# A spectral-mixing FFN kernel: bank rotation in the first FFT, a new order of loads, z in two runs of partitions

## Chip, cores and metric

One Trainium2 chip, one core of it. The metric is the device time of one execution in microseconds (us). A kernel's time is the median of its runs. Times within a run are counted from the start of the profiled span. PE is TensorE, PEld its weight loads, DVE VectorE, ACT ScalarE, POOL GpSimd, SP the engine that issues most transfers. The granted clock is the share of full speed that PE is given; 0.50 is called half clock here. All the runs compared below were in the fast state.

## The reference

```python
X = np.fft.rfft(x, axis=1)                 # x: (8, 3008, 256) float32
Y = X * (filt_r + 1j * filt_i)[None]       # filters: (1505, 256)
y = np.fft.irfft(Y, n=3008, axis=1).astype(np.float32)
h = np.maximum(y.reshape(24064, 256) @ w_in, 0.0)    # w_in: (256, 2048)
out = (h * h @ w_out).astype(np.float32)             # w_out: (2048, 256)
```

## The kernel before

The FFT of length 3008 = 64 x 47 is a chain of matrix products in half precision. **A** makes u from x (47-point part), u goes out to HBM and comes back in another order, **B** does the 64-point part, VectorE multiplies by the filter ("product"), **P** is the inverse 64-point part, z goes out and comes back, **Y** is the inverse 47-point part. **F** brings the filter into the order of B's output by products with permutations. The FFN then runs over 47 groups of 512 tokens, each in 8 slots: a slot does one eighth of the first layer of one group (psH), squares it on VectorE, and one eighth of the second layer of the group before (psO). The FFTs of the seven other batches are laid into these slots by a plan. Only the first batch's FFT stands alone, ahead of the slots; that is the prologue.

The parts that matter (cuts marked `# ...`). Pools first. A pool has slots too, its buffers, which tiles take in turn; these are meant where the text speaks of a slot of a pool, or of a tile's slot. `p_h2` has two of them and many guests, one after the other:

```python
p_h2 = ctx.enter_context(tc.tile_pool(name="p_h2", bufs=2))
# guests of p_h2, in order of their first use: third piece of x(0); u0 (all of u of
# batch 0); f16 (filter in half precision); win32 (first FFN weight, float32);
# wout32 (second FFN weight, float32); from then on the hidden tiles h2

def place_f(im, k, eng):                    # F, one sixth of one filter half
    ps = psH(f"psf_{im}_{k}")               # one of two double banks
    # ... 8 or more permutation products into ps, then one eviction by eng
```

The prologue:

```python
load_f(0)                                   # filt_r, right behind x
# ... constants, chunk_a: A over the same two double banks
chunk_a(0, 0); chunk_a(0, 2); write_u(0, 0); write_u(0, 2)
load_f(1)                                   # filt_i
chunk_a(0, 1); chunk_a(0, 3); write_u(0, 1); write_u(0, 3)
# load sSB; read_u(0); load sSP
f16s.append(p_h2.tile([128, 2, QF + D], F16, tag="h2", name="f16"))
# ... two small casts of the Nyquist row into it, on GpSimd
for im, eng in enumerate((nc.gpsimd, nc.vector)):
    # ... cast filter half im into f16 on eng
    for k in range(6):
        place_f(im, k, nc.vector if k % 2 else nc.scalar)
    keep_warm(12)
# load x(1,0), x(1,1); four half-width swapped copies of sSP on GpSimd; cast x on GpSimd
for r in range(14):
    if r < 12: unit_b(0, r)                 # B and the product
    if r >= 2: unit_p(0, r - 2)             # P; every third one writes a piece of z
    if r == 7: load_win(); cast_win()
for c in range(4): read_z(0, c)             # 96 partitions each
load_wout(); load_x(1, 2); load_x(1, 3)
cast_wout()                                 # four casts on GpSimd
# ... A of x(1,0), x(1,1); casts of x(1,2), x(1,3) on GpSimd
keep_warm(14)
for n in range(16): unit_y(0, n)
```

In the plan for batch b + 1, the casts of its four x pieces are put on VectorE; for batch 2 at slots 31, 33, 35 and 37 of batch 1's plan, each of the first two followed by the request for the next piece but one.

Of the kernel before, what the change touches and what calls it, by code (L numbers as in the profile page):

```python
# [19 lines left out]
QF = 3008  # L20
# [3 lines left out]
def _build_consts():  # L24
# [57 lines left out]

    SY = np.zeros((NC, 2, 2, N2, 2))
    for c in range(NC):
        th = 2 * np.pi * c * n2 / N2
        for i in range(2):
            SY[c, i, 0, :, i] = np.cos(th)
            SY[c, i, 1, :, i] = -np.sin(th)

# [9 lines left out]
    C0[0:94, 576:672] = SA.reshape(94, 96)  # L99
    C0[0:96, 672:766] = SY.reshape(96, 94)  # L100
    return f16(C0, 128), f16(PF, 128), f16(SB, 128), f16(SP, 128)
# [3 lines left out]
def kernel(  # L105
# [34 lines left out]
    p_ze = ctx.enter_context(tc.tile_pool(name="p_ze", bufs=3))  # L140
    p_zt = ctx.enter_context(tc.tile_pool(name="p_zt", bufs=4))
    p_y = ctx.enter_context(tc.tile_pool(name="p_y", bufs=2))
# [17 lines left out]

    prologue = [True]


# [20 lines left out]
    sSA = sC0[0:94, 576:672]  # L184
    sSY = sC0[0:96, 672:766]
    sPF = p_zt.tile([128, 6, 128], F16, tag="zt", name="sPF")
    nc.scalar.dma_start(out=sPF, in_=dPF.ap().rearrange("p (w q) -> p w q", q=128))
# [13 lines left out]
    def load_f(im):  # L201
        filt = filt_i if im else filt_r
        t = p_y.tile([128, QF], F32, tag="yt", name=f"f32_{im}")
        nc.sync.dma_start(out=t, in_=filt[0:1504, :].rearrange("a d -> (a d)").rearrange("(p e) -> p e", e=QF))
        f32s.append(t)

    load_f(0)
    nyq = p_out.tile([128, 2, D], F32, tag="ost", name="nyq")
    nc.gpsimd.memset(nyq, 0.0)
# [23 lines left out]

    def place_f(im, k, eng):

        ps = psH(f"psf_{im}_{k}")
        for i in range(4):
            c = 4 * k + i
            e0, e1 = D * c, D * (47 - c)
            cuts = [0] + [d for d in range(1, D) if (e0 + d) % QF == 0 or (c and (e1 + d) % QF == 0)] + [D]  # L240
            for d0, d1 in zip(cuts, cuts[1:]):
                o = ps[:, i // 2, (i % 2) * D + d0:(i % 2) * D + d1]
                q, a = divmod(e0 + d0, QF)
                nc.tensor.matmul(o, sPF[:, PQ.index((0, q)), :], f16s[0][:, im, a:a + d1 - d0],  # L244
                                 start=True, stop=False)
                q, a = divmod(e1 + d0, QF) if c else (0, QF + d0)
                nc.tensor.matmul(o, sPF[:, PQ.index((1, q)), :], f16s[0][:, im, a:a + d1 - d0],
                                 start=False, stop=True)
        dst = sF[:, im, 4 * k:4 * k + 4, :]
        src = ps.rearrange("p t (a d) -> p (t a) d", d=D)  # L250
        if eng is nc.scalar:
            eng.activation(out=dst, in_=src, func=AF.Copy, scale=sign[:, 0:1] if im else 1.0)
        elif im:
            eng.tensor_scalar_mul(out=dst, in0=src, scalar1=sign[:, 0:1])
        else:
            eng.tensor_copy(out=dst, in_=src)

# [16 lines left out]

    def cast_wout():
        for k in range(4):
            nc.gpsimd.tensor_copy(out=sWout[:, 4 * k:4 * k + 4, :],
                                  in_=w32s[1][:, 4 * k:4 * k + 4, :])

# [30 lines left out]
    def chunk_a(b, c):  # L310
# [6 lines left out]
        for k in range(2):  # L317
            ps = psH(f"psA_{b}_{c}_{k}")
            for i in range(2):
                m = slice(4 * k + 2 * i, 4 * k + 2 * i + 2)  # L320
                o = ps[0:96, i, :]
                if b == 0:
                    nc.tensor.matmul(o, s0[:, c // 2, :], x016[2 * (c % 2)][:, m, :],  # L323
                                     start=True, stop=False)
                    nc.tensor.matmul(o, s0[0:120, 2 + c, :], x016[1][0:120, m, :],  # L325
                                     start=False, stop=True)
                else:
                    nc.tensor.matmul(o, sSA, x16s[(b, c)][:, m, :], start=True, stop=True)
            o = u[:, 4 * k:4 * k + 4, :]
            pv = ps[0:96].rearrange("p t (a d) -> p (t a) d", d=D)  # L330
            if k == 0:
                nc.scalar.copy(out=o, in_=pv)
            else:
                nc.vector.tensor_copy(out=o, in_=pv)

# [33 lines left out]
    def unit_p(b, p):  # L369
# [16 lines left out]
        if i6 == 2:  # L386
            nc.sync.dma_start(
                out=dZ[b].rearrange("(s p) d -> p s d", p=128)[:, 6 * c:6 * c + 6, :],
                in_=zes.pop((b, c)))

    def read_z(b, c):
        zt = p_zt.tile([96, 8, D], F16, tag="zt", name=f"zt_{b}_{c}")
        nc.sync.dma_start(
            out=zt, in_=dZ[b].rearrange("(q j) d -> q j d", j=NM)[:, 8 * c:8 * c + 8, :])
        zts[(b, c)] = zt
# [3 lines left out]
    def unit_y(b, n):  # L399
# [9 lines left out]
        else:  # L409
            if dt == 0:  # L410
                yps[0] = psH(f"psY_{b}_{n}")
            ps = yps[0][:, dt, :]
        for jj in range(4):
            nc.tensor.matmul(ps[:, 94 * jj:94 * jj + 94],  # L414
# [56 lines left out]
    def fft_plan(b):  # L471
# [5 lines left out]

        for a in range(16):
            if b == 1 and a < 8:
                continue  # L480
            r = 2 + a // 2 if b == 1 else a // 2
            put(r, a % 2, unit_a, b, a)
        put(10 if b == 1 else 8, 1, read_u, b)
        for p in range(12):
            r = 14 + p if b == 1 else 13 + 19 * p // 11
            put(r, 0, unit_b, b, p)
            put(r + (b == 1), b == 1, unit_s, b, p)
            put(r + 2 + (b == 1), 1, unit_p, b, p)
        for c in range(4):
# [24 lines left out]
    for k, eng in enumerate((nc.vector, nc.vector, nc.gpsimd)):  # L514
        for i in range(2):
            m = slice(4 * i, 4 * i + 4)
            eng.tensor_copy(out=x016[k][:, m, :], in_=x0[k][:, m, :])
    chunk_a(0, 0)
    chunk_a(0, 2)
    write_u(0, 0)  # L520
    write_u(0, 2)
    load_f(1)
    chunk_a(0, 1)
    chunk_a(0, 3)
    write_u(0, 1)
    write_u(0, 3)
    nc.sync.dma_start(out=sSB, in_=dSB.ap().rearrange("p (a b) -> p a b", b=128))
    read_u(0)
    nc.sync.dma_start(out=sSP, in_=dSP.ap().rearrange("p (a b) -> p a b", b=128))

# [3 lines left out]
    for im, eng in enumerate((nc.gpsimd, nc.vector)):  # L534
        for e in (slice(0, 1504), slice(1504, QF)):
            eng.tensor_copy(out=f16s[0][:, im, e], in_=f32s[im][:, e])
        for k in range(6):
            place_f(im, k, nc.vector if k % 2 else nc.scalar)
        keep_warm(12)
    for c in range(2):  # L540
        load_x(1, c)

    for k in range(2):
        t = p_u.tile([128, 12, 128], F16, tag="u", name=f"sSPx_{k}")
        c = slice(12 * k, 12 * k + 12)
        nc.gpsimd.tensor_copy(out=t[0:64], in_=sSP[64:128, c, :])
        nc.gpsimd.tensor_copy(out=t[64:128], in_=sSP[0:64, c, :])
        sSPx.append(t)
    for c in range(2):
        cast_x(1, c, nc.gpsimd)  # L550
    for r in range(14):
        if r < 12:
            unit_b(0, r)
        if r >= 2:
            unit_p(0, r - 2)
        if r == 7:
            load_win()
            cast_win()
    for c in range(4):
        read_z(0, c)  # L560
    load_wout()
    for c in range(2):
        load_x(1, c + 2)
    cast_wout()
    for c in range(2):
        chunk_a(1, c)
        write_u(1, c)
        cast_x(1, c + 2, nc.gpsimd)
    keep_warm(14)
    for n in range(16):  # L570
# [51 lines left out]
```

## Time and profile before

| | before |
|---|---|
| time, median of 3 runs | 826.12 us (825.33 to 826.16) |
| PE busy in the profiled span of 825.9 us | 793.3 us (96%) |
| first matmul of F | 22.35 us |
| first product of B | 41.74 us |
| last write of z landed | 62.49 us |
| first matmul of Y that uses z | 66.73 us |
| second-layer product of slot 9 | 94.06 us |

The prediction shows the page and the order of instructions of this kernel. Two more pieces are needed later. In a table of busy time by stretch (stretch, length, busy time of PE, PEld, DVE, ACT, POOL with the number of instructions, granted clock, DMA share, GB/s), the 43 us in which F, B and P run:

```profile
19.00:39.00 20.00, 17.78 (x135) 12.37 (x135) 10.52 (x10) 8.43 (x8) 0.00 (x0) 1.00 0.93 314
39.00:62.00 23.00, 17.30 (x106) 9.93 (x103) 17.26 (x15) 8.95 (x14) 11.29 (x8) 1.00 0.71 211
```

And in the order of instructions (start, length, engine, line, operation, tiles, and in brackets the idle time before with what ended it), the casts on GpSimd and the wait of VectorE for x(2,2):

```profile
77.46 4.91 POOL L277 CAST sWout<-wout 128x1024 f16<-128x1024 f32 x4 [13.19 <-DMA wout<-in_moe_w_out_dram]
...
152.03 1.22 DVE L285 CAST x<-x 94x2048 f16<-94x2048 f32 x1 [2.15 <-DMA x<-in_x_dram]
```

PE is busy and at full clock in the first table. The weight's cast waits 13.19 us for a transfer. The last line is VectorE standing 2.15 us at a cast in the middle of the slots.

### The profile page before, as it was taken

Reading aid. Unit: us, or ns where it says so; the run is one execution under the profiler, and the core shown is the slowest. Engines: PE = TensorE matmul, PEld = TensorE weight load, DVE = VectorE, ACT = ScalarE, POOL = GpSimd, SP = SyncE. Lnnn points to the kernel's source line nnn. Section 1 sums busy time; section 2 is a strip of 40 time slices with the busy share of each in tenths; the row PEclk is TensorE's granted clock in tenths of the full one; section 3 lists DMA queues with packets and bytes.
Section 4 is the critical chain, followed back from the end, with each engine's and each line's share of the span. In section 5 each row is a group of like instructions: output and inputs, shape, how many; then the busy total and the mean of one; then the engine's idle time right before and its main releaser. Section 6 shows DMA issues by size and latency. Waiting matters only on the chain.

```text
span 825.9 us, 14241 instructions
## 1 busy us (share of the span) xinstructions
PE 793.3 (96%) x5960; PEld 551.4 (67%) x5960; DVE 551.5 (67%) x861; ACT 548.0 (66%) x695; POOL 50.3 (6%) x53
## 2 busy tenths in 40 slices
PE   6876899999999999999999999999999999999998
PEld 2643466667777676676767776776767767676666
DVE  2573697659965699557975599557985599544432
ACT  2343667677777677676777677776777777666664
POOL 3143263000000000000000000000000000000000
PEclk8996999999999999999999999999999999999999
DMA  7969427544562455334671545534572432411111
GB/s 274 325 205 259 114 92 200 152 130 147 143 169 73 145 154 144 112 99 138 156 208 46 172 122 147 141 84 134 139 185 83 118 120 70 128 40 39 39 39 52
DMA packets 88576, 110.23 MB, mean 133 GB/s; under 512 B 4040, under 2 KB 79560, under 8 KB 83912
## 3 DMA queue, kind: packets, MB, share of 16 engines
q1 hardware_dynamic: 88160, 108.94, 45.4%
q8 instruction: 46, 0.75, 0.4%
q10 hardware_dynamic: 288, 0.39, 0.2%
q14 instruction: 18, 0.15, 0.1%
q0 software_dynamic: 64, 0.00, 0.0%
HBM read 59.51 MB, written 49.81 MB: 132 GB/s over the span
## 4 chain that ended last, share of the span: by engine, by line
PE 85%; DMA 6%; DVE 5%; issue 2%; ACT 1%; SPq 0%; DVEq 0%; ACTq 0%
PE psO L459 37%; PE psH L444 36%; PE psY L414 3%; PE psA L299 3%; DMA x<-in_x_dram 2%; PE psB L346 2%; PE psP L382 2%; DMA zt<-dZ 2%; DVE prod L349 2%; DMA dZ<-ze 1%; DVE h L452 1%; PE psA L323 1%; PE psA L325 1%; DMA ut<-dU 0%; PE psf L244 0%
## 5 line engine op out<-in xcount | busy, mean ns | idle before, releaser
L448 ACT ACTIVATE h<-psH 128x1024 f16<-128x1024 f32 x376 | 385.2, 1025 | 197.9 <-PE psH L444 191.2
L444 PE MATMUL psH<-yt,sWin 128*128 128x512 f16 (+7 forms) x1728 | 389.6, 353 | 0.9 <-DVE yt L423 0.5
L459 PE MATMUL psO<-sWout,h 128*128 128x256 f16 x3008 | 389.5, 273 | 0.0
L459 PEld LDWEIGHTS <-h 128*128 128x128 f16 x3008 | 291.3, 98 | 76.9
L452 DVE TENSOR_TENSOR h<-h 128x1024 f16<-128x1024 f16 x376 | 263.4, 710 | 113.8 <-ACT h L448 113.5
L444 PEld LDWEIGHTS <-sWin 128*128 128x128 f16 x1728 | 160.5, 98 | 106.0 <-issue 8.6
L349 DVE TENSOR_TENSOR prod<-psB,sF 128x1024 f16<-128x1024 f32 x96 | 116.1, 1219 | 6.0 <-PE psB L346 5.2
L384 ACT CAST ze<-psP 128x512 f16<-128x512 f32 x96 | 56.3, 586 | 30.4 <-PE psP L382 17.7
L423 DVE CAST yt<-psY 128x376 f16<-128x376 f32 x64 | 35.2, 549 | 61.1 <-PE psY L414 61.0
L306 DVE CAST u<-psA 96x512 f16<-96x512 f32 x52 | 35.7, 686 | 49.5 <-PE psA L299 49.5
L466 ACT COPY ost<-psO 128x512 f32<-128x512 f32 x94 | 55.3, 589 | 6.8 <-PE psO L459 5.8
L414 PEld LDWEIGHTS <-zt 96*128 96x128 f16 x512 | 36.2, 104 | 25.3 <-DMA zt<-dZ 8.0
L414 PE MATMUL psY<-sC,zt 96*128 96x94 f16 x512 | 42.9, 215 | 9.0 <-DMA zt<-dZ 5.3
L299 PE MATMUL psA<-x,sC 94*96 94x512 f16 x104 | 39.9, 385 | 2.4 <-DVE u L306 2.3
L346 PE MATMUL psB<-ut,sSB 128*128 128x256 f16 x192 | 36.4, 272 | 5.9 <-DVE prod L349 5.2
L346 PEld LDWEIGHTS <-sSB 128*128 128x128 f16 x192 | 18.7, 98 | 29.3 <-issue 10.1
L421 ACT CAST yt<-psY 128x376 f16<-128x376 f32 x64 | 29.9, 467 | 11.7 <-PE psY L414 11.7
L364 DVE TENSOR_TENSOR yf<-prod,yf 128x512 f16<-128x512 f16 x84 | 35.5, 423 | 3.0 <-POOL yf L358 0.5
L382 PE MATMUL psP<-yf,sSP 128*128 128x256 f16 x168 | 32.1, 273 | 0.0
L285 DVE CAST x<-x 94x2048 f16<-94x2048 f32 x24 | 29.2, 1217 | 2.1 <-DMA x<-in_x_dram 2.1
L304 ACT CAST u<-psA 96x512 f16<-96x512 f32 x52 | 29.7, 572 | 0.0
L357 DVE COPY yf<-prod 64x512 f16<-64x512 f16 x72 | 20.8, 289 | 2.5
(48 smaller groups left out, 225.5 us busy)
## 6 DMA issues: line engine op xcount, KB each, us to landing
out_dram<-ost SPq DMA_DIRECT2D x94, 256.0 KB, 3.8
x<-in_x_dram SPq DMA_DIRECT2D x24, 768.0 KB, 6.2
dU<-u SPq DMA_DIRECT2D x32, 384.0 KB, 3.4
dZ<-ze SPq DMA_DIRECT2D x32, 384.0 KB, 2.9
zt<-dZ SPq DMA_DIRECT2D x32, 384.0 KB, 5.9
ut<-dU SPq DMA_DIRECT2D x8, 1024.0 KB, 6.2
ut<-dU SPq DMA_DIRECT2D x8, 512.0 KB, 3.7
x<-in_x_dram SPq DMA_DIRECT2D x3, 1024.0 KB, 7.4
```

Source lines behind the costliest of these rows:

```text
L299: nc.tensor.matmul(ps[0:96, :], sSA, x16s[(b, c)][:, 2 * i:2 * i + 2, :], start=True, stop=True)
L306: nc.vector.tensor_copy(out=o, in_=pv)
L346: nc.tensor.matmul(ps[:, i * D:(i + 1) * D], sSB[:, 2 * p + i, :], uts[b][:, 2 * p + i, :], start=True, stop=True)
L349: nc.vector.tensor_mul(out=prod, in0=ps.rearrange("p (a d) -> p a d", d=D).unsqueeze(1).to_broadcast([128, 2, 2, D]), in1=sF[:, :, 2 * p:2 ...
L382: nc.tensor.matmul(ps[:, i * D:(i + 1) * D], sSP[:, c2, :], prod[:, i, :], start=True, stop=True)
L384: nc.scalar.copy(out=zes[(b, c)][:, 2 * i6:2 * i6 + 2, :], in_=ps.rearrange("p (a d) -> p a d", d=D))
L414: nc.tensor.matmul(ps[:, 94 * jj:94 * jj + 94], zt[:, 4 * (g % 2) + jj, dt * 128:(dt + 1) * 128], sSY, start=True, stop=True)
L444: nc.tensor.matmul(ps[:, i, o:o + n], sWin[:, dt, jt * 128:(jt + 1) * 128], yts[b][:, dt, r:r + n], start=(dt == 0), stop=(dt == 1))
L448: nc.scalar.activation(out=h2[:, 2 * s:2 * s + 2, :], in_=ps, func=AF.Relu)
L452: nc.vector.tensor_mul(out=v, in0=v, in1=v)
L459: nc.tensor.matmul(pso[g][:, t % 2, :], h2s[g][:, jt, t * 128:(t + 1) * 128], sWout[:, jt, :], start=(jt == 0), stop=(jt == NJT - 1))
L466: nc.scalar.copy(out=ost, in_=pso[g])
```

## The change

The intent: keep PE from waiting for evictions in the prologue (four pairs of banks in rotation), have all of F's input ahead of u on the queue, spread the constants and weights so that what is needed first comes first, take the second weight's casts from GpSimd to VectorE slot by slot, read z onto partitions 0 to 47 and 64 to 111, and fill Y's waits with products by zeros. The diff, cut:

```diff
+    def bank_pair(name):          # double banks of psH twice, then psF pair, psO pair
+        k = npair[0] % 4
+        # ... A (chunk_a) and F (place_f) take their banks from here and evict
+        #     in turn by ScalarE and VectorE
     load_f(0)
+    load_f(1)
-    chunk_a(0, 0); chunk_a(0, 2); write_u(0, 0); write_u(0, 2); load_f(1); ...
+    for c in (0, 2, 1, 3):
+        chunk_a(0, c)
+        write_u(0, c)
+    # sSB and sSP loaded in halves: SB0, SP0, read_u(0), SB1, SP1
+    load_win()
+    for c in range(2):
+        load_x(1, c)
     f16s.append(p_h2.tile([128, 2, QF + D], F16, tag="h2", name="f16"))
     # ... filter casts and F, as before
-        keep_warm(12)
-    for k in range(2):                       # swapped copies of sSP
+    for k, eng in enumerate((nc.vector, nc.gpsimd)):
-        nc.gpsimd.tensor_copy(...)  # twice
+        eng.tensor_copy(...)        # twice
+    cast_win()
-        if r == 7: load_win(); cast_win()
-    cast_wout()                              # GpSimd
+    # plan of batch 1: cast_wout(k) on VectorE at slots 2 to 5, x(1,2), x(1,3) cast
+    # on VectorE at slots 6 and 7; A, read_u, B a slot later
-    keep_warm(14)
+    keep_warm(12)
     def read_z(b, c):
-        one transfer onto 96 partitions
+        for k in range(2):
+            nc.sync.dma_start(out=zt[64 * k:64 * k + 48],
+                              in_=v[48 * k:48 * k + 48, 8 * c:8 * c + 8, :])
     # Y contracts over 112 partitions (16 of them zeros); in unit_y:
+        if prologue[0]:
+            nc.tensor.matmul(ps[:, 0:D], zero[:, 0:128], zero[:, 0:D], start=True, stop=True)
```

## The prediction

> **What bounds the kernel now.** I read the page first, then the table of busy time by stretch, the order of instructions of the first 110 us, and the waits. The page's slices and the table say where time can be lost at all:
>
> ```profile
> PE   6876899999999999999999999999999999999998
> PEclk8996999999999999999999999999999999999999
> ```
>
> ```profile
> 62.00:67.00 5.00, 0.27 (x4) 0.27 (x5) 0.00 (x0) 0.00 (x0) 2.27 (x3) 0.94 0.68 169
> 67.00:75.00 8.00, 5.76 (x64) 4.97 (x63) 3.94 (x8) 3.78 (x8) 0.00 (x0) 0.50 1.07 296
> 81.00:90.00 9.00, 6.12 (x26) 2.36 (x25) 8.64 (x8) 6.17 (x8) 5.96 (x4) 1.00 0.42 119
> ...
> 150.00:300.00 150.00, 148.73 (x1161) 104.48 (x1159) 108.30 (x178) 107.03 (x139) 0.00 (x0) 1.00 0.46 131
> 300.00:500.00 200.00, 199.77 (x1543) 143.25 (x1542) 149.37 (x250) 144.31 (x185) 0.00 (x0) 1.00 0.49 136
> ```
>
> (Stretch, its length, busy time of PE, weight loads, VectorE, ScalarE, GpSimd, granted clock, DMA share, GB/s.) From 150 us on PE is busy 99 to 100% at full clock. The change adds no PE work there: the products with zeros are issued in the prologue alone, and contracting over 112 instead of 96 rows streams the same 94 columns. So all that can move lies in the first 100 us: the first batch's forward FFT (stages A, F and B), its inverse (P, the z read, Y), and the first eight half-filled FFN slots. The order of instructions there:
>
> ```profile
> 14.48 0.74 POOL L533 CAST f<-nyq 128x256 f16<-128x256 f32 x2
> ...
> 22.35 0.27 PE L244 MATMUL psf<-f,sPF 128*128 128x256 f16 x1
> ...
> 30.73 0.81 SPq L340 DMA_DIRECT2D ut<-dU  x2
> ...
> 41.74 13.67 DVE L349 TENSOR_TENSOR prod<-psB,sF 128x1024 f16<-128x1024 f32 x12 [1.59 <-PE psB L346]
> ...
> 62.63 1.73 SPq L393 DMA_DIRECT2D zt<-dZ  x4
> ...
> 66.73 1.12 PE L414 MATMUL psY<-sC,zt 96*128 96x94 f16 x12 [4.87 <-DMA zt<-dZ]
> ...
> 81.36 6.74 DVE L452 TENSOR_TENSOR h<-h 128x1024 f16<-128x1024 f16 x4 [0.88 <-ACT h L448]
> ...
> 94.06 1.04 PE L459 MATMUL psO<-sWout,h 128*128 128x256 f16 x8
> ```
>
> The reader should see four things. F (line 244) starts at 22.3, right behind A. The twelve products of B take 13.7 us on VectorE in one piece, so VectorE, not PE, paces B and P. PE then waits 4.87 us for z. And four squarings that cost 0.69 us each are spread over 6.74 us at 81 us, while GpSimd casts the second weight and x. The last line is the second-layer product of slot 9; from there slots follow at some 1.75 us, as in the steady state. I measure the prologue to this point.
>
> **What the Trainium skill says.** (1) "TensorE: Matmul & The Clock Gate", Part 1: the clock falls to half after about 3.4 us of idling and rises after about 3.4 us of sustained work. The trace agrees: the 128x512 matmuls of A follow each other at 0.22 us, then at 0.43 us, after the idling from 6.3 to 10.6 us; the clock of 67 to 75 us is 0.50 after the wait for z. (2) "SBUF — State Buffer", "Who interferes with whom": a VectorE instruction with two SBUF inputs blocks against a GpSimd instruction that reads SBUF. The stretched squarings beside GpSimd casts agree. (3) The same page, "Can I just issue two DMAs to hit both halves?", answers no (two transfers at partitions 0 and 64 gained 6%). The trace has only the single-piece form: 128-row reads ran at some 400 GB/s, the 96-row z read at some 255. Whether two runs of 48 help is not shown here.
>
> **The change, part by part.** All times are from the start of the span.
>
> *A over four bank pairs.* Before, PE waited for the eviction of the pair in use (1.31 us at 14.05), and that gap seems to have kept the clock at half until 18.6. With four pairs the gap goes. A's first product with both inputs stays at 10.6, since it waits for x. 32 matmuls: about 20 at 0.43 and the rest at 0.22 at worst, and at best half of them slow; PE ends A about 19 to 20 instead of 22.2, the last eviction about 20.5 instead of 23.6. The evictions of split pairs are 2 x 0.57 us (ScalarE) or 2 x 0.69 us (VectorE) for 1.01 and 1.22: no bound.
>
> *Filter loads ahead of u.* The first filter half landed at 15.9, and the second, 1.54 MB at the 400 GB/s that the queue showed, would be in at 19.5 instead of 28.4. The four u writes (0.39 MB, about 1.1 us each in line) follow it and have landed about 24.5. Before, the read of u waited for them until 30.7. So u is in SBUF 6 us earlier, at about 30.5. But that is not what sets B's start.
>
> *The weights' buffer.* This is the step that I rate highest. The first FFN weight is now requested before the half-precision filter copy, from the same two-slot pool. The slot that came free first, that of the third x piece, now goes to the weight; the filter copy gets the slot of u, free only once all u writes have landed. Before, the filter cast at 14.48 began as soon as the x cast had ended, which agrees with its having that slot. So F can start at 24.5 + 0.74 + 2.83 (two filter casts of GpSimd, from the groups) = 28.1, not 22.35: 5.8 us later. PE idles from 20 to 28 and comes back at half clock.
>
> *F itself.* 54 matmuls per filter half: 42 x 0.108 and 12 short ones make 5.2 us at full clock, and with four pairs the evictions (1.02 to 1.28 us, alternating between two engines) keep up. First half: 5.2 + 2.0 for the cold stretch, to 35.3. Then, as before, VectorE must evict its last block (1.3) and cast the second filter (2 x 0.93), to 38.5; the dummy matmuls that filled this gap are gone, so the second half may start cold: 5.2 + 1.5, to 45.2. Last eviction 1.4 and the two swapped weight copies now on VectorE, some 0.9: the first product is at 47.5 instead of 41.7. **Lost: 5.8 us.**
>
> *B, P, z.* Twelve products 13.7 us, to 61.2; 1.3 more to the last z write (as before, 55.4 to 56.7), at 62.5. That write took 5.76 us before because the weight load was ahead of it on the queue; this load now runs near 35 us, so I take the usual 2.9: 65.4. Reading z: 4.05 us to the first tile, as before (twice as many issues, half the bytes each). Y starts at 69.5 instead of 66.7. **Net loss to here 2.8 us.**
>
> *From Y to slot 9.* Before, 94.06 - 66.73 = 27.3 us. The fillers make Y longer while cold (16 x 0.088 + 4 x 0.216 + a wait of 0.56 = 2.8 us per four units, against 1.97) and shorter later; I take 8 us for 8.7. The casts that blocked VectorE leave GpSimd: 4 x 0.65 us for the second weight and 2 x 1.22 for x, in VectorE's own order. The new limit is VectorE after the second weight has landed. Before, it landed 77.4 - 62.6 = 14.8 us after the z read's issue, so 10.8 us after Y's start. From there: 4 x 0.65 + 6 squarings x 0.69 + 2 x 1.22 + 0.69 = 9.9, so slot 9 has its input about 20.9 us after Y's start. **Gain 27.3 - 20.9 = 6.4 us.**
>
> Sum: -6.4 + 2.8 = -3.6 us, from 826.1 to 822.5. Everything after that is shifted whole, as PE is full.
>
> **Rivals.** *F is not held by u.* If the filter copy gets a free slot after all, F starts at 20 and ends by 34, u is there at 30.5, the first product is at 35 instead of 41.7, and with the shorter z write Y starts at 57 to 60. With the gain after Y the time would be 811 to 813. For it: the change is plainly meant to do this. Against it: the slot order above. *The cold clock eats it.* If F runs cold in both halves and B after it too (1.3 us a step for the 1.14 that VectorE sets), the first product is at 49 to 50 and Y at 71 to 73; 825 to 827. For it: three pieces of dummy work are removed just where PE now idles longest. *Two runs of 48 change z's rate.* At 400 GB/s in place of 255 the z data would be in 2.3 us sooner, so also the second weight and x behind it: 820. If instead each run is confined to half the ports, with about 3 us more, 825.5; the steady state could hide either, as z is asked for four slots ahead. *The wait moves to the second weight.* VectorE, in order, may stand at its cast from slot 2 on; I counted this, but if the x pieces behind it land 3 us later still, slot 9 slips and the time is 825.
>
> **Range and chances.** The late F, the clock and the z rate each carry 2 to 3 us, mostly independent: 822.5 with 815.5 to 828 for 8 in 10, stretched downwards for the first rival. Over 2% faster means under 809.6, which needs that rival and luck besides: 0.05. Over 2% slower means over 842.6, for which I see no mechanism, since the steady state isn't touched: 0.01. Within 2%: 0.94.
>
> **What would show it.** The first filter cast on GpSimd begins about 24.5, released by a u write; F's first matmul at 28. The first product of B at 46 to 49, the first Y matmul at 68 to 71, slot 9's second-layer product about 90.5; no stretched squarings at 81 to 88, but a wait of VectorE for the second weight. The prediction is wrong if F starts before 24, if Y starts before 64, or if the PE share after 150 us changes.

## The result, and the profile after

The changed kernel took **832.28 us** (median of 4 runs, 831.21 to 833.49) beside 826.14 us of the kernel before (4 runs) on the same chip: ratio 1.0069, interval 1.0042 to 1.0096. A ratio here is the mean time of one kernel's fast runs over that of the other's of the same rounds, so it is not quite the ratio of the medians quoted. By the 2% rule this is "the same". But the kernel became slower by 6 us, where 4 us of gain were predicted, and the time lies outside the predicted range.

The same views of the changed kernel. Page, slices of 20.8 us:

```profile
PE   6566899899999999999999999999999999999997
...
PEclk9789999999999999999999999999999999999999
```

Busy time by stretch, columns as above:

```profile
19.00:39.00 20.00, 8.96 (x58) 6.58 (x57) 6.02 (x8) 3.24 (x4) 6.45 (x6) 0.74 1.00 352
39.00:62.00 23.00, 14.61 (x116) 11.34 (x114) 20.90 (x19) 8.92 (x14) 8.00 (x6) 0.85 0.34 85
62.00:67.00 5.00, 3.16 (x18) 1.69 (x17) 3.43 (x5) 3.64 (x6) 0.00 (x0) 1.00 0.53 147
67.00:75.00 8.00, 5.23 (x48) 3.10 (x48) 2.23 (x4) 1.89 (x4) 0.00 (x0) 1.00 0.83 187
81.00:90.00 9.00, 6.58 (x28) 2.58 (x27) 5.55 (x9) 7.74 (x8) 0.00 (x0) 1.00 1.05 271
150.00:300.00 150.00, 147.41 (x1148) 103.04 (x1146) 103.92 (x171) 104.26 (x136) 0.00 (x0) 0.99 0.47 131
```

From 19 to 39 us PE works 8.96 us instead of 17.78: F is late. The stretch from 150 us on has lost 1.3 us of PE work too, which the prediction had ruled out. The order of instructions shows where:

```profile
25.11 0.75 POOL L570 CAST f<-nyq 128x256 f16<-128x256 f32 x2 [10.60 <-DMA dU<-u]
...
27.29 0.37 PE L261 MATMUL psf<-f,sPF 128*128 128x256 f16 x1 [8.28 <-POOL f L573]
...
45.44 4.06 POOL L304 CAST x<-x 94x2048 f16<-94x2048 f32 x2
45.48 2.26 DVE L580 COPY sSPx<-sSP 64x1536 f16<-64x1536 f16 x1
47.75 2.15 DVE L581 COPY sSPx<-sSP 64x1536 f16<-64x1536 f16 x1
49.94 10.27 DVE L371 TENSOR_TENSOR prod<-psB,sF 128x1024 f16<-128x1024 f32 x9
...
71.42 0.33 PE L445 MATMUL psY<-sC,zt 112*128 112x94 f16 x4 [1.52 <-DMA zt<-dZ]
...
85.84 0.69 DVE L296 CAST sWout<-wout 128x1024 f16<-128x1024 f32 x1 [2.19 <-DMA wout<-in_moe_w_out_dram]
...
91.93 0.92 PE L318 MATMUL psA<-x,sC 94*96 94x512 f16 x2 [3.67 <-DVE x L304]
...
97.30 1.04 PE L490 MATMUL psO<-sWout,h 128*128 128x256 f16 x8
...
157.72 1.22 DVE L304 CAST x<-x 94x2048 f16<-94x2048 f32 x1 [4.66 <-DMA x<-in_x_dram]
```

Five things: the first filter cast waits 10.60 us and a write of u releases it; the two swapped copies on VectorE take 2.26 and 2.15 us while GpSimd casts x and weights; the first product is at 49.94 (before 41.74); VectorE waits for the second weight until 85.84; and at 157.72 it has stood 4.66 us at the cast of x(2,2), in the middle of the slots.

| us from the start | before | after | difference |
|---|---|---|---|
| first matmul of F | 22.35 | 27.29 | +4.94 |
| first matmul of F's second half | 31.83 | 38.52 | +6.69 |
| first product of B | 41.74 | 49.94 | +8.20 |
| last write of z landed | 62.49 | 68.13 | +5.64 |
| first matmul of Y on z | 66.73 | 71.42 | +4.69 |
| second-layer product of slot 9 | 94.06 | 97.30 | +3.24 |
| of slot 36 | 151.65 | 154.82 | +3.17 |
| of slot 40 | 161.66 | 168.10 | +6.44 |
| of slot 383, the last | 820.93 | 826.29 | +5.36 |
| end of the span | 825.93 | 831.71 | +5.78 |

The difference is made in two places: before slot 9, and between slots 36 and 40. This is one execution; two repeats of the same kernel (numbers 1 and 16) had their first product at 50.95 and 48.75 and took 11.53 and 12.05 us from slot 36 to 40, where this one took 13.28.

### The profile page after: what moved, and what is told of

The parts are those of the page before. It is cut to its first block, busy times and chain, and to the rows that moved or that the text cites. A ratio compares the mean times of both kernels' runs of the same rounds, so it can differ in the third digit from the quotient of the medians.

```text
span 831.7 us, 14317 instructions
## 1 busy us (share of the span) xinstructions
PE 788.6 (95%) x5950; PEld 550.8 (66%) x5950; DVE 560.0 (67%) x879; ACT 548.4 (66%) x701; POOL 38.2 (5%) x45
## 4 chain that ended last, share of the span: by engine, by line
PE 87%; DMA 5%; DVE 4%; issue 2%; SPq 0%; POOL 0%; ACT 0%; DVEq 0%; POOLq 0%; ACTq 0%
PE psO L490 38%; PE psH L475 37%; PE psA L318 3%; DMA x<-in_x_dram 2%; PE psB L368 2%; PE psY L445 2%; PE psP L404 2%; DMA wout<-in_moe_w_out_dram 2%; DVE prod L371 2%; PE psf L264 1%; PE psf L261 1%; DMA dU<-u 1%; DVE h L483 1%; PE psA L344 1%; DMA ut<-dU 0%
## 5 line engine op out<-in xcount | busy, mean ns | idle before, releaser
L483 DVE TENSOR_TENSOR h<-h 128x1024 f16<-128x1024 f16 x376 | 259.0, 697 | 110.6 <-ACT h L479 110.3
L445 PEld LDWEIGHTS <-zt 112*128 112x128 f16 x512 | 35.8, 98 | 23.2 <-issue 9.0
L445 PE MATMUL psY<-sC,zt 112*128 112x94 f16 x512 | 42.3, 206 | 4.3 <-DVE yt L454 2.0
L304 DVE CAST x<-x 94x2048 f16<-94x2048 f32 x26 | 31.6, 1217 | 4.7 <-DMA x<-in_x_dram 4.7
L261 PE MATMUL psf<-f,sPF 128*128 128x256 f16 (+3 forms) x54 | 13.6, 299 | 10.5 <-POOL f L573 8.3
```

Source lines behind the costliest of these rows:

```text
L445: nc.tensor.matmul(ps[:, 94 * jj:94 * jj + 94], zt[:, 4 * (g % 2) + jj, dt * 128:(dt + 1) * 128], sSY, start=True, stop=True)
L483: nc.vector.tensor_mul(out=v, in0=v, in1=v)
```

## The experiments

Two theories at first. **S** (slot): the filter copy sits in the slot of u and so must wait for u's writes; this sets F and all behind it. **Z**: z in two runs of 48 partitions comes in more slowly and holds back all that is queued behind it, the second weight and x. A third cost to be measured was the swapped copies on VectorE.

### 1. Name the filter copy's tile before the weight's

```diff
# changed kernel
+    f16s.append(p_h2.tile([128, 2, QF + D], F16, tag="h2", name="f16"))
     load_win()
     ...
-    f16s.append(p_h2.tile([128, 2, QF + D], F16, tag="h2", name="f16"))
```

> The changed kernel, with only the filter copy's buffer requested before the first weight's, so that it gets the slot of the third x piece again and not that of u. Theory S (the filter copy waits for u's slot, and this is what costs the prologue): GpSimd's first filter cast starts at about 14.5 instead of 25.1 us, F's first matmul about 19 instead of 28.6, the first product of B about 35 instead of 49.9, the first product of Y about 57 instead of 71.4; the time falls by some 13 to 15 us to 817 to 819, under the kernel before (826). Rival C (the swapped copies on VectorE and their fight with GpSimd are the cost): F is earlier, but VectorE still stands some 4 us at the copies; 826 to 829. Rival Z (the z read in two runs is the cost): F is earlier but the loss after Y stays and nothing before it shows; 830 to 832.

Measured: 833.75 us (4 runs) beside 825.13; ratio 1.0109. F at 27.17, first product at 50.95. **The experiment failed as an experiment**: in this program a slot is given at a tile's first use, not where it is named, and the first use had not moved. So it says nothing on S; it is a repeat of the changed kernel.

### 2. z in one run again

```diff
# changed kernel: SY of 96 rows, z tiles [96, 8, D] without zeros
-        for k in range(2):
-            nc.sync.dma_start(out=zt[64 * k:64 * k + 48], in_=v[48 * k:48 * k + 48, ...])
+        nc.sync.dma_start(out=zt, in_=v[:, 8 * c:8 * c + 8, :])
```

> The changed kernel with z read in one run of 96 partitions, as before, and Y contracting over 96 rows. Rival Z: the loss of 3.3 us that the changed kernel shows at slots 37 to 39 (a cast of x that waits for its load behind z) vanishes, and the second weight lands 2 to 4 us sooner after Y's start; time 826 to 829. Theory S: the prologue up to the last z write stays as it is (first product of B at 49 to 51 us); if S is all there is, the time stays at 832 within 1 us.

Measured: 830.27 us (5 runs), ratio 1.0058. Y starts at 71.52 (changed 71.42), the second weight is cast from 86.13 (85.84), slots 36 to 40 still take 12.87 us (13.28; before 10.01). In this trace nothing that Z should mend is mended. The two runs of the changed kernel do come more slowly: one 192 KB piece per 1.02 to 1.05 us is some 190 GB/s, where one 384 KB run took about 1.5 us, some 255 GB/s. By time, though, this run is 3.5 us below number 1, which is the changed kernel on the same chip in the same rounds, and the intervals (1.0040 to 1.0077 here, 1.0093 to 1.0124 there) don't touch. The profiled execution was the slowest of the five (837.47 us, the others 828.57 to 831.84), so the trace can't show where that came from. **Z sets neither F nor the first product; that it has a part in the loss is not excluded.** Number 7 asks again on a better kernel.

### 3. Both swapped copies on GpSimd

```diff
# changed kernel
-    for k, eng in enumerate((nc.vector, nc.gpsimd)):
+    for k, eng in enumerate((nc.gpsimd, nc.gpsimd)):
```

> The changed kernel with both pairs of swapped weight copies on GpSimd, as before. Rival C: VectorE no longer spends 2.26 and 2.15 us on the first pair beside GpSimd's casts; the first product of B at about 45.5 instead of 49.9 us, all later stages 4.4 us earlier, time about 828. Theory S alone: the copies lay in time that VectorE lost anyway; the first product stays near 50 and the time at 832.

Measured: 827.93 us (5 runs), ratio 1.0045; the first product at 45.65, 4.29 earlier than in the changed kernel, for the 4.41 us that the copies took on VectorE. Y started at 67.74, 3.68 earlier. Then PE ran Y at half clock (from 68.5 to 82.2), Y took 10.60 us instead of 7.96, and slot 9 is 3.63 earlier. Beside number 1, the changed kernel on the same chip, the run is 5.8 us shorter, and the intervals (1.0027 to 1.0064, 1.0093 to 1.0124) don't touch. So the copies cost some 4 to 6 us of what the changed kernel lost. (Y at half clock isn't the edit's doing: see number 9.)

### 4. The weight's load ahead of the filter copy, in the kernel before

```diff
# kernel before
+    load_win()
     f16s.append(p_h2.tile([128, 2, QF + D], F16, tag="h2", name="f16"))
 ...
-            load_win()
             cast_win()
```

> The kernel before with one line moved: the first weight's buffer and load are requested before the filter copy's buffer, so the filter copy gets u's slot. Theory S: GpSimd's first filter cast waits for the last u write, about 30.7 us instead of 14.5; F's first matmul about 34 instead of 22.3, first product of B about 53 instead of 41.7, time up by 8 to 12 us to 834 to 838 (some 3 us come back because the last z write no longer queues behind the weight). If S is wrong: F stays at 22 to 24 and the time within 3 us of 826.

Measured: **837.43 us** (4 runs), ratio 1.0150, interval 1.0130 to 1.0170. This moves only that request, and the guests of the two slots change places. The order of instructions:

```profile
31.19 0.75 POOL L534 CAST f<-nyq 128x256 f16<-128x256 f32 x2 [16.97 <-DMA dU<-u]
...
33.37 0.37 PE L244 MATMUL psf<-f,sPF 128*128 128x256 f16 x1 [10.70 <-POOL f L537]
```

The cast has stood for 16.97 us and a write of u ends it, where it began at 14.48 in the kernel before. F starts 11.02 later, slot 9 is 9.86 later. **S holds**, and the damage can be made in the kernel before by itself.

### 5. The filter copy's first use ahead of the weight's load

```diff
# changed kernel
+    f16s.append(p_h2.tile([128, 2, QF + D], F16, tag="h2", name="f16"))
+    for i in range(2):
+        nc.gpsimd.tensor_copy(out=f16s[0][:, i, QF:], in_=nyq[:, i, :])
     load_win()
     ...
-    f16s.append(...)      # and its two Nyquist casts, at the old place
```

> The first try left the slots as they were, because a slot is given at a buffer's first use and not where it is named. Here the two small casts that use the filter copy first stand ahead of the load of the first weight in program order, so the copy does get the third x piece's slot (the built program says so). Theory S: filter casts on GpSimd from about 14.3 us, F's first matmul about 19, the first product of B at 35 to 38, the first product of Y at 57 to 60; time 817 to 821. Rival (F's place is not what bounds; u's arrival, the weights or GpSimd are): F earlier, but the first product at 45 or later and the time over 826.

Measured: **818.58 us** (4 runs, 813.58 to 819.05) beside 827.02; ratio 0.9885, interval 0.9847 to 0.9924. Three lines moved are worth some 13.7 us against the changed kernel (medians on two chips).

```profile
14.21 0.75 POOL L566 CAST f<-nyq 128x256 f16<-128x256 f32 x2
15.73 2.82 POOL L573 CAST f<-f 128x1504 f16<-128x1504 f32 x2 [0.77 <-DMA f<-in_filt_r_dram]
...
32.82 0.56 DVE L580 COPY sSPx<-sSP 64x1536 f16<-64x1536 f16 x1
33.39 0.55 DVE L581 COPY sSPx<-sSP 64x1536 f16<-64x1536 f16 x1
33.97 13.66 DVE L371 TENSOR_TENSOR prod<-psB,sF 128x1024 f16<-128x1024 f32 x12
```

The filter cast now waits for the filter (0.77 us), F starts at 17.22 and the first product is at 33.97, 15.97 earlier than in the changed kernel. And the same two swapped copies take 0.56 and 0.55 us: GpSimd is idle then, its casts of the weight come at 42.45. So the loss of experiment 3 was a consequence of F's lateness, which pushed the copies onto GpSimd's casts.

### 6. That, and the copies on GpSimd

Experiment 5's edit and experiment 3's together; call it **the mended kernel**.

> The same and both pairs of swapped weight copies on GpSimd. With F early, VectorE wants its pair at about 34 us, when GpSimd copies its own: if the two fight over it as in the changed kernel, this run's first product is 1 to 3 us earlier than the last one's, and the time as much lower. If the fight was only with the casts of the first weight and of x, which come later now, the two runs are equal within 1 us.

Measured: 817.19 us (4 runs), ratio 0.9879, interval 0.9848 to 0.9910. Medians differ by 1.4 us from experiment 5 and the intervals nearly coincide: with the slot mended, the copies' engine hardly matters.

### 7. The mended kernel with z in one run

Experiment 2's edit on the mended kernel.

> The last with z read in one run of 96 partitions. Rival Z (two runs read slower: 190 GB/s in the changed kernel against 250): the last z piece lands about 2 us sooner after its request, the second weight too, and the time falls 1 to 4 us. Against it: the second x cast's wait at slots 36 to 38 stayed in the first one-run experiment, so the time may not move by more than 1 us.

Measured: 820.14 us (7 runs, 816.29 to 823.92), ratio 0.9919, interval 0.9890 to 0.9947, overlapping that of the mended kernel on the same chip. The second weight's cast starts at 72.46 (73.25), slots 36 to 40 take 13.11 us (11.58). No gain from one run on this kernel; a small loss can't be told from none (the profiled execution was again the slowest, 823.92).

### 8. The mended kernel with all first runs of z asked for before the second

```diff
# mended kernel, in read_z: called once for all four tiles
+            for i in range(4):
+                nc.sync.dma_start(out=ztiles[i][64 * k:64 * k + 48], ...)   # k = 0, then k = 1
```

> Instead, z in two runs, but all four first runs are requested before the four second ones. The first run needs only the first two writes of z, so four of the eight pieces can be read while the last products are still made. If the z read bounds what follows, the last z piece lands 3 to 4 us sooner after the last z write, Y's first product stays or comes up to 2 us later, the second weight lands 3 us sooner, and the time falls 2 to 4 us against the interleaved order. If it doesn't bound, no change.

Measured: **847.71 us** (4 runs), ratio 1.0242. The first tile is complete only after five transfers instead of two: Y starts at 60.73 instead of 57.09. The bulk of the loss is in the slots: from slot 108 to 383 it takes 544 us instead of 524, and the granted clock falls to half five times there, some 99 us apart. The order in which z's pieces are asked for is worth more in the steady state than in the prologue.

### 9. The mended kernel without the products with zeros in Y

```diff
-        if prologue[0]:
-            nc.tensor.matmul(ps[:, 0:D], zero[:, 0:128], zero[:, 0:D], start=True, stop=True)
```

> The repaired kernel (filter copy in its old slot, both swapped copies on GpSimd; 817.2 us) without the products with zeros in Y. There Y ran at half clock and took 10.6 us. If the fillers only lengthen a cold Y: Y takes 8 to 8.7 us as in the kernel before, and the time falls by up to 2 us. If they are what brings the clock back (in the repaired run at 71.8 us, 14 us after it fell), the clock stays low into the first FFN slots, slot 9 comes later, and the time rises by 1 to 3 us.

Measured: 815.34 us (5 runs) beside 825.52; ratio 0.9902, interval 0.9867 to 0.9936, so the same as the mended kernel by ratio. In the traces Y takes 8.41 us instead of 10.61, both at half clock for the most part. The zeros did not bring the clock back sooner in this pair: in the mended kernel PE was busy in 11.30 of the 13.70 us from 58.1 to 71.8 and the granted clock was 0.50 throughout; without the zeros it was back at 67.47. But Y's clock changes from one execution to the next: in 7 of the 16 traces with zeros Y ran wholly at full clock (changed kernel: 7.96 us, number 1: 8.22) and in the others mostly at half (number 16, the same kernel: 10.61); in the four traces without zeros it never ran wholly at full clock. Whether the zeros help to keep the clock up is open. It didn't bring slot 9 nearer in the three traces of the changed kernel: 25.9 and 25.6 us from Y's start at full clock, 26.0 at half. No gain in time from the zeros is seen (see 18).

### 10. The mended kernel with the casts back on GpSimd

```diff
# mended kernel: cast_wout, and the casts of x(1,2) and x(1,3), as in the kernel before
-        nc.vector.tensor_copy(out=sWout[:, 4 * k:4 * k + 4, :], ...)
+        nc.gpsimd.tensor_copy(out=sWout[:, 4 * k:4 * k + 4, :], ...)
```

> The repaired kernel with the casts of the second weight and of x pieces 2 and 3 on GpSimd in one piece, as before the change. The step of the prediction: VectorE's squarings then stretch beside GpSimd's casts, slot 9 comes some 4 to 6 us later after Y's start, time 820 to 823. Rival: since the second weight lands 16 us after Y's start anyway, it's the landing that counts and not the engine; within 1.5 us of 817.

Measured: 818.93 us (6 runs), ratio 0.9922, interval 0.9897 to 0.9948.

```profile
71.25 5.82 POOL L296 CAST sWout<-wout 128x1024 f16<-128x1024 f32 x4 [22.23 <-DMA wout<-in_moe_w_out_dram]
72.38 3.80 DVE L483 TENSOR_TENSOR h<-h 128x1024 f16<-128x1024 f16 x3 [0.53 <-ACT h L479]
```

The squarings are stretched again (3.80 us for three of 0.69), and from Y's start to slot 9 it takes 28.2 us instead of 25.9. Y ran at full clock here and at half in the mended kernel; in numbers 5 and 18, with the casts on VectorE and Y at full clock, it takes 26.8 and 27.0. So the move of the casts to VectorE is worth 1 to 2 us there by the traces; the times agree in sign (818.93 against 817.19), but the intervals overlap, so this is not settled.

### 11. The mended kernel with two pairs of banks for A and F, as before the change

```diff
-        k = npair[0] % 4
+        k = 0
```

(With `k` at 0 every tile comes from psH, which has two double banks.)

> The repaired kernel with A and F on two double banks again (engines alternate as before). If the four pairs are worth what they show: A's last matmul at 21 to 22 instead of 18.7 us, each F half 1.5 us longer, first product of B at 37 to 39 instead of 34.8, time 819 to 821. Rival: u's arrival near 32 us and the swapped copies near 31 hold B, so the first product moves by less than 1 us and the time not at all.

Measured: 823.06 us (20 runs), ratio 0.9975, interval 0.9961 to 0.9990. F ends at 40.38 instead of 33.86 and the first product is at 41.62 instead of 34.78. **The rotation over four pairs is worth some 4 to 8 us** once F isn't held by its copy's slot: 5.9 by the medians and 0.0096 of 826 us by the ratios (two chips), 6.8 at the first product and 4.3 at the end of the traces. Two things blur the size. VectorE's casts of the filter's second half took 3.49 us here, beside a swapped copy on GpSimd, where they took 1.78, so some 1.7 of the 6.8 are not the banks themselves. And slot 9 is only 2.4 later: Y ran at full clock, the second weight was cast from 12.6 us after Y's start (mended kernel 16.2), and slot 9 came 22.4 us after Y's start (25.9).

### 12. The mended kernel with the second weight asked for before the last two writes of z

```diff
+        if r == 7:
+            load_wout()
...
-    load_wout()
```

> The repaired kernel with the second weight's load requested before the last two z writes instead of after the z read. If its landing is what bounds from Y to slot 9: VectorE's first cast of it comes with slot 2, without a wait, x's pieces land 6 us sooner, slot 9 comes 3 to 6 us sooner after Y's start, against some 2 to 3 us for z writes that queue behind it; time 812 to 816. If that landing does not bound: Y is 2 to 3 us later and the time 818 to 820.

Measured: 822.24 us (20 runs), ratio 0.9953.

```profile
60.48 0.47 PE L445 MATMUL psY<-sC,zt 112*128 112x94 f16 x4 [5.79 <-DMA zt<-dZ]
...
77.05 0.69 DVE L296 CAST sWout<-wout 128x1024 f16<-128x1024 f32 x1
```

The weight's cast no longer waits for a transfer, yet it starts at 77.05, later than in the mended kernel (73.25), since Y starts 3.39 later behind the weight's transfer, runs wholly at half clock, and VectorE takes its work in order. From Y's start to slot 9: 26.4 us, against 25.9. So **the landing of the second weight is not the only bound of that stretch**.

### 13. The casts of x(2,2) and x(2,3) two slots later

The second place, slots 36 to 40. In the changed kernel VectorE waited 4.66 us for x(2,2) there.

```diff
# changed kernel, plan of batch 1
-                put(r, 1, cast_x, b + 1, c)
+                put(r + (2 if b == 1 and c > 1 else 0), 1, cast_x, b + 1, c)
```

> The changed kernel with the casts of the two pieces x(2,2) and x(2,3) placed two slots later in VectorE's order, nothing else. In the changed kernel VectorE stood 4.66 us at the first of these casts and second-layer slots 36 to 40 took 13.3 us, against 10.0 us before. Theory: that wait sits in the path and is the 3.3 us that the prediction did not foresee; then slots 36 to 40 take 10 to 11 us and the time is near 829 us. Rival: PE then waits for the piece itself when its own slot needs it, or the stall only moves; then the time stays near 832 us.

Measured: 828.54 us (22 runs) beside 825.40; ratio 1.0041, interval 1.0024 to 1.0058. Slots 36 to 40 take 8.89 us instead of 13.28. The interval overlaps that of the changed kernel, run on another chip, so 16 and 17 repeat the pair side by side.

### 14. The best version: mended, no zeros, later casts

Experiments 6, 9 and 13 together.

> The best kernel so far (filter copy with a slot that is free early, swapped copies on GpSimd, no zero products in Y: 815.3 us) with the casts of x(2,2) and x(2,3) two slots later. If the wait for these pieces still costs something there: 813 to 815 us. If not: 815 us.

Measured: **813.16 us** (6 runs, 810.14 to 814.41) beside 825.40; ratio 0.9842, interval 0.9814 to 0.9870. It beats both kernels: 1.6% faster than the kernel before. Slots 36 to 40 take 8.89 us (10.55 in experiment 9).

### 15. The mended kernel with the filter's second half back behind u

```diff
     load_f(0)
-    load_f(1)
 ...
         write_u(0, c)
+        if c == 2:
+            load_f(1)
```

> The mended kernel (filter copy with a slot that is free early, swapped copies on GpSimd: 817.2 us) with the second half of the filter's load back in its old place on the queue, after the second write of u. If it matters once F is no longer held by the copy's slot that the filter is wholly ahead of u, the second half lands some 9 us later, F's second half and the first product come later by some us and the time is 818 to 823 us. If the second half's load is hidden by F's first half: 817 us, and the z run starts no later.

Measured: 818.63 us (6 runs), ratio 0.9912, interval 0.9885 to 0.9939. F's second half starts at 26.46 (26.25 in the mended kernel), the first product is at 34.97 (34.78). **"F wholly ahead of u" is hidden**: its later landing is covered by F's first half. A difference below the intervals' width stays possible, but the path to the first product shows 0.2 us.

### 16 and 17. The changed kernel again, and with the later casts, side by side

Number 16 is the changed kernel without an edit, 17 is number 13 again.

> The changed kernel unaltered, so that the later casts can be compared with it on one chip and in the same rounds. 832 to 834 us; VectorE stands 4 to 5 us at the cast of x(2,2) and slots 36 to 40 take 13 us.

> The changed kernel with the casts of x(2,2) and x(2,3) two slots later, beside the unaltered one. If the wait for x(2,2) is worth what the slots show (13.3 us against 8.9 for slots 36 to 40): 4 us less than the unaltered one, so 828 to 830 us. If the stretch only moves: the same as the unaltered one within 1 us.

Measured in the same rounds: 832.97 us (6 runs, 831.46 to 834.28), ratio 1.0100, interval 1.0076 to 1.0123, and 829.77 us (7 runs, 828.05 to 830.75), ratio 1.0052, interval 1.0033 to 1.0071. VectorE at the cast of x(2,2), first of number 16:

```profile
156.86 1.22 DVE L304 CAST x<-x 94x2048 f16<-94x2048 f32 x1 [4.62 <-DMA x<-in_x_dram]
```

then of number 17:

```profile
158.19 1.22 DVE L304 CAST x<-x 94x2048 f16<-94x2048 f32 x1 [0.25 <-DMA x<-in_x_dram]
```

The two differ by 3.2 us in the median, and slots 36 to 40 take 12.05 and 8.89 us, 3.16 apart. **The unforeseen loss is this wait**, and it is not only moved. Against the kernel before (10.01 us there, with a wait of its own) the loss is smaller, 1.5 to 3.3 us in the three traces of the changed kernel. Number 17 is within 4.2 us of the kernel before (825.6).

The trace of number 16 shows two more things of the unedited changed kernel, the swapped copies beside GpSimd's casts of x, and PE's wait for a cast of x before slot 9:

```profile
43.95 1.89 POOL L304 CAST x<-x 94x2048 f16<-94x2048 f32 x1
46.00 0.56 DVE L580 COPY sSPx<-sSP 64x1536 f16<-64x1536 f16 x1
46.34 1.97 POOL L304 CAST x<-x 94x2048 f16<-94x2048 f32 x1 [0.50 <-DMA x<-in_x_dram]
46.57 2.15 DVE L581 COPY sSPx<-sSP 64x1536 f16<-64x1536 f16 x1
...
92.72 0.59 PE L318 MATMUL psA<-x,sC 94*96 94x512 f16 x2 [1.40 <-DVE x L304]
```

The first copy starts while GpSimd is idle and takes 0.56 us; the second starts inside a cast and ends only after it, 2.15 us. So the copies cost 2.71 us here, where they cost 4.41 in the first trace.

### 18. The best version with the products with zeros kept

Number 14 without the edit of number 9.

> The mended kernel with the later casts, and with the products with zeros in Y kept, which the best version left out. If the products with zeros do nothing: 813 us, as without them (813.2). If they lengthen Y by the 2 us that the earlier pair of traces showed and this is on the path: 815 us.

Measured: 814.86 us (5 runs), ratio 0.9879, interval 0.9855 to 0.9903, against 0.9842 (0.9814 to 0.9870) without them. The sign agrees with number 9 by the medians, not by its ratios; the intervals overlap, so a loss of 1 to 2 us by the zeros is possible but not settled, and a gain isn't seen.

## Why the prediction was wrong

The prediction said 822.5 (815.5 to 828) and the kernel took 832.3. Its sum had three terms: a net loss of 2.8 us to the start of Y, a gain of 6.4 us from there to slot 9, nothing afterwards. Measured: a loss of 4.7, a gain of 1.4 (25.9 us against 27.3), and a further loss of 2.5 (3.3 at slots 36 to 40, of which 1.1 came back by slot 383, and 0.4 at the end). That is 4.7 - 1.4 + 2.5 = 5.8 us, the difference of the two spans. Two slips in the prediction's working changed nothing: 10.8 + 9.9 is 20.7 and not 20.9, and PE's idling from 6.3 to 10.6 us in the kernel before is broken by one matmul at 7.68.

**Right: the slot.** "F can start at 28.1": it started at 27.29, released by a write of u, and experiments 4 and 5 show this from both sides. The step also named what proved the largest cause: undoing it alone (number 5) turns 832.3 into 818.6. The end of A, "about 19 to 20", was 19.01; F's second half began at 38.52 ("38.5") and F's last matmul was at 44.46 ("45.2").

**Right in size: B to z.** The twelve products took 13.66 us ("13.7") and the last z write was issued 1.32 us behind them ("1.3"). It landed after 3.21 us ("2.9") and the first tile of z 3.29 us later ("4.05"), since the first run of it needs only the first two writes and was asked for ahead.

**Wrong, first step: "the two swapped weight copies now on VectorE, some 0.9".** They took 4.41 us (2.69 and 2.71 in the repeats, numbers 1 and 16), so the first product was at 49.94 instead of 47.5; the rest of that step was even 1.1 us too long. Alone they take 1.11 us (number 5), so 0.9 was a fair duration for the copies alone. What failed is that they weren't looked at in the place where the predicted lateness of F would put them: beside GpSimd's casts of the first weight and x, at 41.5 to 49.5. The prediction had quoted the rule, Trainium skill, "SBUF — State Buffer", "Who interferes with whom", for instructions with two SBUF inputs; the same section says that VectorE contends with GpSimd in its two-port modes too, which copies can enter, and that whoever issues first holds the ports for its whole instruction while the other is blocked. The traces agree: 0.56 us grows to 2.26 beside the casts, and in number 16 one copy took 0.56 us before a cast and the next 2.15 inside it. Moving them off VectorE alone brings the first product to 45.65 (number 3).

**Wrong, second step: "Gain 27.3 - 20.9 = 6.4 us".** The second weight landed 14.4 us after Y's start, where the step took over 10.8 from the kernel before. 1.0 of the 3.6 us is that Y started sooner after the last z write (3.29 us against 4.24); 2.7 is that the weight came later after it (17.7 us against 15.0). From there to slot 9 it took 11.5 us instead of 9.9: PE waited 3.67 us, to 91.93, for a cast of x that stood behind the weight's, and the clock was at half from 92.06 to 95.47. In number 16, the same kernel, that wait was 1.40 us, the clock stayed up and this part took 9.8 us, as the step had it. But there Y ran at half clock, VectorE came to the weight only 16.2 us after Y's start, without a wait, and slot 9 was as late (26.0 us after Y's start). So the step overlooked a second bound: in that execution the weight's landing isn't what is waited for, nor in the mended kernel's trace, where the first cast comes 16.2 us after Y's start too. Why the weight's transfer takes longer is **open**: with z in one run it was no faster (number 2: landed 9.35 us after the last z tile; changed kernel 8.45, before 6.1). Asking for the weight sooner did not help, as it made Y later and Y ran at half clock (number 12). Only number 11 had both, Y at full clock and the weight cast 12.6 us after Y's start, and there slot 9 came after 22.4 us, near the 20.9 of the step.

**Wrong, third step: "Everything after that is shifted whole, as PE is full."** PE is full there only as long as VectorE keeps its order. At slot 36 VectorE stands at the cast of x(2,2), and the evictions of Y behind it wait; so does PE, for 1.97 us at one place, and the clock is at half from 160.3 to 163.7. The wait was in the kernel before as well, 2.15 us long: slots 36 to 40 took 10.01 us there and 8.89 where the cast is later. In the changed kernel the piece lands 13.9 us after the last z write of that batch, where it was 11.8 before: z in eight pieces takes 9.6 us instead of 8.9, and x behind it 4.35 instead of 2.85. With z in one run it was 13.2, so z's two runs are at most a part of it; the rest is open. The cost of the wait itself is shown: 3.2 us against later casts (numbers 16 and 17).

**The rivals.** "F is not held by u" (811 to 813) was rightly put aside for this kernel; where it is made true the time is 817.2 to 818.6, and 813.2 with the best of the rest. "The cold clock eats it": B began at half clock (47.7 to 54.5), but VectorE paced it, 13.66 us as before. "Two runs change z's rate": the rate did fall, to some 190 GB/s, and the time followed by 3.5 us at most (number 2 beside number 1), not at all on the mended kernel (number 7). "The wait moves to the second weight" came true in part: it names the wait at 85.84, though the edit that removed that wait (number 12) gained nothing.

So the change holds one part that gains once the slot is right (the four pairs of banks, some 4 to 8 us), one that may (the casts on VectorE, 1 to 2 between Y and slot 9, not settled), one that is hidden (the filter ahead of u), one that gains nothing and may have cost some us in the changed kernel (z in two runs), and one order of requests that costs more than all of them.

## What to carry to other kernels

A tile that moves ahead in program order takes a different slot of a shared pool, and what it displaces inherits another tile's wait: write down the guests of each slot, before and after, by first use. When a step is predicted late, go through everything that was to run at that moment and ask what it now runs beside; a copy that is cheap alone can cost four times as much there. And a cast that an in-order engine must wait for belongs as late as its reader allows, even in a stretch where the matmul engine is 99% busy.

## What the Trainium skill lacked or had wrong

- "SBUF — State Buffer", "Can I just issue two DMAs to hit both halves?": it gives +6% for two transfers at partitions 0 and 64 over a single one. It doesn't set them beside one transfer that covers both halves. Here two runs of 48 partitions at 0 and 64, asked for one after the other, brought some 190 GB/s against some 255 GB/s for one run of 96.
- "TensorE: Matmul & The Clock Gate", Part 1: full clock after some 3.4 us of sustained work. It doesn't say how much of that time must be busy. In the mended kernel PE was busy 11.30 of 13.70 us (82%) and stayed at half clock throughout.
- No page that I read says what a tile that takes over a slot of a shared pool inherits; here it was worth some 13.7 us (832.3 against 818.6).
